# Layer two's seven products in pairs: a fourth bank, a split x-by-keys product, key sums gated on GpSimd, four kept sums moved

## The chip, the cores and the metric

One core of a Trainium2 chip runs the kernel. Its engines have queues of their own and wait for each other through semaphores: PE (TensorE; its weight loads are listed as PEld), DVE (VectorE), ACT (ScalarE), POOL (GpSimd) and SP (SyncE, which here only issues DMAs). The metric is the device time of one execution in microseconds, the median over runs. Matmul sums lie in eight PSUM banks of 128x512 float32; everything else lies in SBUF.

## What is computed

Two layers with the same weights. Each is a linear-attention block and a gated MLP with token mixing, on 2048 tokens (16 tiles of 128) of 512 features:

```python
def _A_ref(x, wqkv, wo):                       # H = 32 heads of 16
    q, k, v = ...                              # from x @ wqkv
    phi = lambda t: where(t > 0, t + 1, exp(t)) + 1e-6
    pq, pk = phi(q), phi(k)
    kv = einsum("bhsd,bhse->bhde", pk, v)
    z = einsum("bhsd->bhd", pk)
    num = einsum("bhqd,bhde->bhqe", pq, kv)
    den = einsum("bhqd,bhd->bhq", pq, z)[..., None] + 1e-6
    return (num / den) @ wo
def _B_ref(x, w_in, w_sp, b_sp, w_out):
    z = gelu(x @ w_in)
    z1, z2 = z[..., :896], layernorm(z[..., 896:])
    return (z1 * (w_sp @ z2 + b_sp)) @ w_out
x = x + _A_ref(layernorm(x), ...)
x = x + _B_ref(layernorm(x), ...)              # and both once more
```

## The kernel before

Every float32 product is done as three matmuls on high and low parts (`mm3`): high by high, high by low, low by high. A split into parts is an ACT copy that rounds (the high part, L136) and a DVE subtraction (the low part, L139). All engines follow the order in which the program is written.

The stages are, for each layer: keys, queries and the x-by-keys product (class `P1`), a transition, the rest of attention and the MLP's inputs (`P2`), and the token mixing with the output (`P4`). The change lies in layer two's `P1`, and in the loops ahead of and behind it.

**Layer two's pairs.** Tiles 0 to 9 go in five pairs (`pair`, p = 0 to 4). For a pair of tiles a and b, the product of 256 rows with the key and query weights is done by Winograd's seven products of half size, P1 to P7, each of six matmuls. Before, they use three banks: A (P1, then P2 on top), E (P7, then P4 on top) and B (an ACT copy of A, L897, then P6, P5, P3 on top). w is a copy of E taken before P4, u a copy of B taken after P6. The four quarters of keys and queries are A, X = w + B after P5 (written into bank A, L948), B after P3, and E + u (written into E, L975). From each, `pair_phi` (two ACT operations, Relu L868 and Exp L869) and `pair_out` (two DVE operations of 128x256, L879) make the key half `r` and the query half. A tile's keys are then split (`K_high` ACT L569, `K_low` DVE L574), added up on GpSimd (L578), and multiplied with the tile's x, split by `x_high` and `x_low`, in `Gmm`: twelve matmuls onto four banks G that stay through the stage. So three product banks, four G banks and one more make eight. Tiles of pair p get their `Gmm` in pair p+1. The next pair's operands are made in this pair: two stream transposes (`rows`, L448), four half-size sums (`pair_sums`), and three splits into xA (`first_part`), xB (`second_part`) and xS (`sum_part`); xD (`last_part`) is split at the pair's own start. The last of the five pairs prepares tile 10 instead, and tiles 10 to 15 follow one by one in `second`.

**Kept sums.** Token mixing's nested product N4 needs 16 sums of blocks of w_sp, made ahead of time (`Inner`), each by a DVE addition (L1694 to L1704), an ACT high part, a DVE low part and DMAs. `begin` sets how many are due, each call of `staged` moves the pipeline on by one. Eight of N4's are made in layer one's last loop (`join`, which runs once for each of 16 tiles i, at i = 3 to 6 and 12 to 15), four in pairs 1 to 4, four in layer two's mixing. The sums of N1 are made in layer two's `P2.run`, from step s = 6 on.

**Weights of P4.** In pair 0, `joint.parts(m, j, (4,))` splits the weight operand of the product P4: four ACT and four DVE operations of 128x256.

## Time and profile before

| | |
|---|---|
| median of 3 runs | 1385.57 us (1384.47 to 1385.74) |
| the profiled execution | 1386.03 us, its span 1384.0 us |
| PE busy | 1354.5 us (98%) |
| DVE busy | 1067.9 us (77%) |
| ACT busy | 658.1 us (48%) |
| POOL busy | 509.4 us (37%) |
| layer two's pairs and the hand-over to single tiles | 692.6 to 797.3 us of the span |

A row of the timeline has the start, the duration, the engine, the line, the operation, its tiles (out<-in) and shapes; in brackets stands how long the engine was idle before it and what released it. Consecutive matmuls overlap: their spacing, not their duration, is what each takes of PE. A row of the windows has a stretch and its length, then the busy time (with the number of instructions) of PE, PEld, DVE, ACT and POOL, then the granted TensorE clock, the DMA engines' busy share and GB/s.

### The profile page before, as it was taken

The numbers are of one execution on the slowest core, as the hardware profiler recorded it, in microseconds if no ns is written. First come the engines' busy times: TensorE is split into PE (matmuls) and PEld (weight loads), VectorE is DVE, ScalarE is ACT, GpSimd is POOL, SyncE is SP. The second block draws the span as 40 slices with busy tenths as digits, with TensorE's granted clock in tenths as the row PEclk, the third lists the DMA queues.
The fourth block names the chain that finished last, engine by engine and source line by source line (L and its number), as shares of the span: only waits on it lengthen the run. The fifth ranks groups of instructions, "written<-read, shape, count | busy, mean of one in ns | idle before, by whom it ended". The sixth has DMA issues, their size and how long they took to land. (4 is left out here: it accounts for less than half of the span.)

```text
span 1384.0 us, 18449 instructions
## 1 busy us (share of the span) xinstructions
PE 1354.5 (98%) x6055; PEld 1126.0 (81%) x6055; DVE 1067.9 (77%) x1670; ACT 658.1 (48%) x1066; POOL 509.4 (37%) x600
## 2 busy tenths in 40 slices
PE   9999999999999999999978899999999999999998
PEld 6888888888888888887756688888888888888887
DVE  7985887876866898978968777877777698878642
ACT  7875543345443343434456665544456534533410
POOL 3343476533483357327412224633240011312340
PEclk9999999999999999999989999999999999999999
DMA  5762479866797988869653442656567798668652
GB/s 189 230 205 88 137 258 321 294 205 207 266 333 263 311 285 283 301 257 308 223 187 101 128 147 77 217 181 226 191 204 247 232 347 312 206 197 297 230 185 88
DMA packets 181743, 310.16 MB, mean 224 GB/s; under 512 B 15696, under 2 KB 67920, under 8 KB 177552
## 3 DMA queue, kind: packets, MB, share of 16 engines
q1 hardware_dynamic: 166544, 251.45, 55.4%
q0 software_dynamic: 11504, 51.12, 10.2%
q10 hardware_dynamic: 3600, 6.42, 1.3%
q8 instruction: 47, 0.77, 0.2%
q14 instruction: 48, 0.39, 0.1%
HBM read 211.68 MB, written 97.26 MB: 223 GB/s over the span
## 5 line engine op out<-in xcount | busy, mean ns | idle before, releaser
L1973 PE MATMUL bank<-qd,pg 128*128 128x512 f32 x544 | 211.6, 389 | 0.0
L1974 PE MATMUL bank<-qd,pg 128*128 128x512 f32 x544 | 211.6, 389 | 0.0
L1975 PE MATMUL bank<-qd,pg 128*128 128x512 f32 x544 | 211.6, 389 | 0.0
L1820 DVE TENSOR_TENSOR qd<-qd,qd 128x1024 fp32r<-128x1024 f32 x104 | 140.9, 1355 | 67.8 <-ACT qd L1811 67.3
L1811 ACT ACTIVATE qd<-qd 128x1024 fp32r<-128x1024 f32 x104 | 110.1, 1058 | 129.6 <-DMA qd<-s 43.9
L136 ACT ACTIVATE pg<-pg 128x512 fp32r<-128x512 f32 (+1 forms) x146 | 88.3, 612 | 109.8 <-DVE pg L448 30.3
L380 POOL TENSOR_SCALAR rs<-mv 128x1 f32<-128x1 f32 x96 | 41.8, 436 | 258.1 <-DVE mv L375 244.2
L1995 POOL TENSOR_TENSOR bg<-bg,pg 128x512 f32<-128x512 f32 x56 | 91.2, 1641 | 109.2 <-DMA pg<-z 102.3
L139 DVE TENSOR_TENSOR pg<-pg,pg 128x512 fp32r<-128x512 f32 (+1 forms) x143 | 112.7, 789 | 20.9 <-ACT pg L136 17.9
L1974 PEld LDWEIGHTS bank<-qd,pg 128*128 128x128 f32 x544 | 102.1, 188 | 21.4
L1975 PEld LDWEIGHTS bank<-qd,pg 128*128 128x128 f32 x544 | 102.1, 188 | 21.2
L1973 PEld LDWEIGHTS bank<-qd,pg 128*128 128x128 f32 x544 | 102.1, 188 | 21.1
L152 PE MATMUL bank<-qd,pg 128*128 128x512 f32 x300 | 117.4, 391 | 0.5 <-DVE pg L139 0.5
L1563 POOL TENSOR_TENSOR pg<-pg,pg 128x512 f32<-128x512 f32 x50 | 78.3, 1567 | 104.6 <-DMA pg<-in_wsp_dram 82.1
L448 DVE STREAM_TRANSPOSE pg<-pg 128x512 f32<-128x512 f32 x79 | 86.0, 1088 | 11.3 <-DMA pg<-yt 9.5
L150 PE MATMUL bank<-bg,qd 128*128 128x448 f32 x256 | 94.0, 367 | 0.0
L151 PE MATMUL bank<-bg,qd 128*128 128x448 f32 x256 | 93.6, 366 | 0.0
L152 PE MATMUL bank<-bg,qd 128*128 128x448 f32 x256 | 93.4, 365 | 0.0
L152 PE MATMUL bank<-wo,qd 128*128 128x512 f32 x224 | 88.0, 393 | 3.2 <-DVE qd L139 3.1
L151 PE MATMUL bank<-wo,qd 128*128 128x512 f32 x224 | 87.2, 389 | 0.0
L150 PE MATMUL bank<-wo,qd 128*128 128x512 f32 x224 | 87.2, 389 | 0.0
L1904 PE MATMUL bank<-qd,pg 128*128 128x512 f32 x224 | 87.1, 389 | 0.0
(289 smaller groups left out, 3362.5 us busy)
## 6 DMA issues: line engine op xcount, KB each, us to landing
qd<-s SPq DMA_DIRECT2D x64, 512.0 KB, 4.2
qd<-n POOLq DMA_DIRECT2D x32, 1024.0 KB, 8.9
pg<-in_wsp_dram SPq DMA_DIRECT2D x96, 256.0 KB, 4.9
qd<-in_wsp_dram SPq DMA_DIRECT2D x40, 512.0 KB, 4.3
n<-pg SPq DMA_DIRECT2D x68, 256.0 KB, 4.3
pg<-z SPq DMA_DIRECT2D x56, 256.0 KB, 4.7
x<-pg SPq DMA_DIRECT2D x48, 256.0 KB, 2.9
pg<-x SPq DMA_DIRECT2D x48, 256.0 KB, 3.9
```

The costliest lines, as they stand in the source:

```text
L136: nc.scalar.activation(h, src, AF.Copy)
L139: nc.vector.tensor_sub(l, src, h.bitcast(F32))
L150: nc.tensor.matmul(out, ah, bh, start=start, stop=False)
L151: nc.tensor.matmul(out, ah, bl, start=False, stop=False)
L152: nc.tensor.matmul(out, al, bh, start=False, stop=stop)
L1811: nc.scalar.activation(wh, r, AF.Copy)
L1820: nc.vector.tensor_sub(wl, r, wh.bitcast(F32))
L1904: m(out[i], h[:, o, f], w[:, o, 0], start=first and name in ("P1", "P2", "P5"), stop=False, skip_group_check=True)
L1973: m(out, h[:, o], w[:, 0, j, :], start=start, stop=False, skip_group_check=True)
L1974: m(out, h[:, o], w[:, 1, j, :], start=False, stop=False, skip_group_check=True)
L1975: m(out, l[:, o], w[:, 0, j, :], start=False, stop=stop, skip_group_check=True)
L1995: nc.gpsimd.tensor_tensor(u, u, z1, op=OP.mult)
```

## The change

It does seven things. (1) X gets a bank of its own, so PE may write the other banks sooner; the quarter E + u goes to an SBUF tile c, and E's bank is released at once. (2) The order of the products becomes P1, P7, P2, P6, P5, P4, P3 in pairs 1 to 4 and P1, P7, P6, P2, P5, P4, P3 in pair 0: P4 stands between P5 and P3, and P3's quarter is left for the next pair. (3) `Gmm` of the tile that is finished last is cut in halves: two of its four banks between P5 and P4, the other two in the next pair between P7 and P2. (4) The key sums leave `K_low` in pairs 1 to 4; they are issued by `zsum` behind a GpSimd operation of 128x1 (`wait_for`; in pair 4 only the first of the two has one) that reads what DVE has just written, ahead of a transposition on DVE. The first transposition of a pair has the sum of tile b of the pair before, the second that of tile a. (5) The low part of a piece of the output weights goes from GpSimd (L144) to DVE. (6) P4's weight operand is split in `join` at i = 15, and tile 15's normalised rows are made and sent later in pair 0. (7) Four of N4's kept sums go from i = 3 to 6 of `join` to s = 3 to 6 of layer two's `P2.run`, and N1's start one step later there.

```diff
-        def Gmm(self, i):
+        def Gmm(self, i, cs=range(4), first=None):
...
+            if cs[-1] < 3:
+                self.xhl[i] = h, l
+                return
             pages.put(h, l, *self.pk.pop(i))
...
+        def wait_for(self, t):
+            s = small.tile([P, 1], F32, name="after")
+            nc.gpsimd.tensor_scalar(s, t if t.dtype == F32 else t.bitcast(F32), 1.0, None, op0=OP.mult)
+        def zsum(self, i):
+            r = self.r.pop(i)
+            if self.zacc is None:
+                self.zacc = r
+            else:
+                nc.gpsimd.tensor_tensor(r, self.zacc, r, op=OP.add)
+                pages.put(self.zacc, lag=POOL)
+                self.zacc = r
+        def key_low(self, i):
+            h, l = self.pk[i]
+            nc.vector.scalar_tensor_tensor(l, self.r[i], PHI_EPS, h.bitcast(F32), op0=OP.add, op1=OP.subtract)
...
             B = banks.get(PAGE)
+            if p:
+                c, r, last = self.open
+                self.pair_out(c, r, b - 2, 0)
+                self.K_high(b - 2)
             nc.scalar.activation(B, A, AF.Copy)
+            self.last_part(p)
             if p:
-                self.K_high(a - 2)
...
+                r = self.pair_phi(last)
+                self.key_low(b - 2)
+                self.x_high(b - 2)
+                self.x_low(b - 2)
...
             nc.scalar.activation(w, E, AF.Copy)
             if p:
-                self.keys(b - 2)
-            else:
-                for m in range(2):
-                    for j in range(2):
-                        self.joint.parts(m, j, (4,))
-                        self.joint.done(m, j + 2)
-            if p:
+                self.pair_out(last, r, a - 2, 1)
+                banks.put(last)
+                self.K_high(a - 2)
+                self.key_low(a - 2)
+                if p > 1:
+                    self.Gmm(a - 4, (2, 3), False)
                 self.product(A, "P2", p)
             self.product(B, "P6", p)
...
+                self.pair_out(A, r, a, 0)
+                self.Gmm(b - 2, range(4), p == 1)
+                self.x_high(a - 2)
+                self.x_low(a - 2)
+                self.wait_for(self.xhl[a - 2][1][:, 0:1])
+                self.zsum(b - 2)
...
                 self.first_part(nxt)
+                if p:
+                    self.wait_for(self.ops[nxt, "A"][1][:, 0, 0:1])
+            if p:
+                self.zsum(a - 2)
+            self.product(B, "P5", p)
+            X = banks.get(PAGE)
+            nc.vector.tensor_add(X, w, B)
+            r = self.pair_phi(X)
...
+            if p:
+                self.Gmm(a - 2, (0, 1), False)
+            lows = deque()
             if p and side:
-                side.popleft().piece(True)
+                side.popleft().piece(lows=lows)
...
+            self.product(E, "P4", p)
+            nc.vector.tensor_add(c, E, u)
+            banks.put(E)
             self.product(B, "P3", p)
-            r = self.pair_phi(B)
-            self.product(E, "P4", p)
-            self.pair_out(B, r, a, 1)
-            banks.put(B)
-            nc.vector.tensor_add(E, E, u)
-            self.open = E, b
+            self.open = c, self.pair_phi(c), B
+            for l, src, h, t in lows:
+                low(l, src, h)
+                pages.put(t)
+            own.staged(False)
...
-                elif s == 5:
-                    own.begin(2)
-                elif 6 <= s:
-                    own.staged()
+                else:
+                    if s == 2:
+                        inner["N4"].begin(1, 1)
+                    elif 2 < s < 10:
+                        inner["N4"].staged(s < 7)
+                    if s == 6:
+                        own.begin(2)
+                    elif s > 6:
+                        own.staged()
...
-            if i == 2:
-                inner["N4"].begin(2, 1)
-            elif 2 < i < 10 or i > 11:
-                inner["N4"].staged(i < 7 or i > 11)
+            if i == 11:
+                inner["N4"].begin(1, 1)
+            elif i > 11:
+                inner["N4"].staged()
+            if i == 15:
+                for m in range(2):
+                    for j in range(2):
+                        w.parts(m, j, (4,))
+                        w.done(m, j + 2)
```

Three places of the engines' orders follow. ACT at the start of pair 0, before (L897 is the copy of A to B, bg and qd of 128x256 are P4's weight parts, w and u the copies of E and B):

```order
L136 ACTIVATE pg_730_7025<-pg_719_6890 128x512
L897 ACTIVATE bank_182_7047<-bank_180_7033 128x512
L394 ACTIVATE pg_733_7049<-pg_720_6892,nb,rs 128x4x4x32
L136 ACTIVATE pg_734_7051<-pg_710_6782 128x256
L136 ACTIVATE qd_159_7028<-pg_728_6983 128x512
L915 ACTIVATE w_7060<-bank_181_7040 128x512
L136 ACTIVATE qd_160_7062<-pg_665_6275 128x256
L136 ACTIVATE qd_160_7062<-pg_679_6395 128x256
L136 ACTIVATE qd_160_7062<-pg_666_6277 128x4x2x32
L136 ACTIVATE qd_160_7062<-pg_680_6397 128x4x2x32
L931 ACTIVATE u_7077<-bank_182_7047 128x512
L868 ACTIVATE pg_735_7085<-bank_180_7033 128x512
```

and now (L922 is the copy of A to B, L930 writes w, L951 u, L871 is the Relu):

```order
L136 ACTIVATE pg_720_6991<-pg_709_6856 128x512
L136 ACTIVATE qd_159_6994<-pg_665_6275 128x256
L136 ACTIVATE qd_159_6994<-pg_677_6391 128x256
L136 ACTIVATE qd_159_6994<-pg_666_6277 128x4x2x32
L136 ACTIVATE qd_159_6994<-pg_678_6393 128x4x2x32
L922 ACTIVATE bank_182_7022<-bank_180_7008 128x512
L136 ACTIVATE pg_723_7024<-pg_698_6744 128x256
L930 ACTIVATE w_7027<-bank_181_7015 128x512
L951 ACTIVATE u_7035<-bank_182_7022 128x512
L871 ACTIVATE pg_724_7043<-bank_180_7008 128x512
```

The four parts of P4's weights moved from between w and u to ahead of the copy of A; tile 15's normalisation (L394) and a kept sum's high part (qd of 128x512) left this place. ACT at the start of pair 2, before (bank_185 and bank_192 are B of pairs 1 and 2):

```order
L868 ACTIVATE pg_774_7308<-bank_185_7176 128x512
L869 ACTIVATE pg_774_7308<-pg_774_7308 128x512
L897 ACTIVATE bank_192_7340<-bank_190_7326 128x512
L569 ACTIVATE pg_778_7342<-pg_760_7220 128x512
L136 ACTIVATE pg_780_7345<-pg_763_7244 128x256
```

and now (c is E + u of pair 1, bank_186 its B):

```order
L871 ACTIVATE pg_763_7280<-c_7272 128x512
L872 ACTIVATE pg_763_7280<-pg_763_7280 128x512
L569 ACTIVATE pg_768_7309<-pg_759_7251 128x512
L922 ACTIVATE bank_194_7306<-bank_192_7292 128x512
L136 ACTIVATE pg_770_7313<-pg_753_7211 128x256
L871 ACTIVATE pg_771_7316<-bank_186_7142 128x512
L872 ACTIVATE pg_771_7316<-pg_771_7316 128x512
```

The Relu and Exp of the old B moved behind the copy, those of c ahead of it, and the key's high part (L569) now stands ahead of the copy. GpSimd from pair 1 on, before (L144 is the weights' low part):

```order
L578 TENSOR_TENSOR pg_743_7122<-pg_736_7088,pg_743_7122 128x512
L144 TENSOR_TENSOR bg_14_7281<-pg_748_7156,bg_13_7280 128x512
L578 TENSOR_TENSOR pg_760_7220<-pg_743_7122,pg_760_7220 128x512
L578 TENSOR_TENSOR pg_769_7286<-pg_760_7220,pg_769_7286 128x512
L144 TENSOR_TENSOR bg_14_7281<-pg_775_7320,bg_13_7280 128x512
```

and now:

```order
L892 TENSOR_SCALAR after<-pg_752_7206 128x1
L892 TENSOR_SCALAR after<-pg_754_7215 128x1
L899 TENSOR_TENSOR pg_725_7046<-pg_733_7086,pg_725_7046 128x512
L892 TENSOR_SCALAR after<-pg_779_7372 128x1
L899 TENSOR_TENSOR pg_759_7251<-pg_725_7046,pg_759_7251 128x512
```

The weights' low parts are gone from it, and each key sum has an operation of one column ahead of it.

72 lines of the change are left out of this document (28 added, 44 removed).

## The prediction

> **What bounds the kernel now.** I read the page's totals first, then PE's waits, then busy time by stage. The number of matmuls does not change, so the time moves only by what PE idles and by the clock it gets.
>
> ```profile
> PE   1354.5 (98%) x6055; PEld 1126.0 (81%) x6055; DVE 1067.9 (77%) x1670; ACT 658.1 (48%) x1066; POOL 509.4 (37%) x600
> ...
> PE bank L802 <- DVE bank L948: 9.4, 4, 6.7
> PE bank L152 <- DVE pg L139: 5.3, 5, 1.5
> ...
> PE bank L802 <- ACT u L931: 2.2, 1, 2.2
> ```
>
> Some 29.5 us of 1384.0 are not PE's. The waits (us in total, times, longest) name the place: L802 is a matmul of the seven products, L948 the addition that makes X, L931 the copy u of pair 0, L152 (here) the third matmul of a `Gmm` or of a tile's keys. The windows give it by stage; the rows are layer one's last loop, pairs 0, 1, 2 and 3, pair 4 with the hand-over, the rest, and steps 3 to 5 of layer two's `P2`.
>
> ```profile
> 634.00:692.60 58.60, 55.41 (x237) 43.61 (x236) 53.56 (x93) 27.07 (x42) 30.53 (x39) 1.00 0.76 252
> 692.60:714.40 21.80, 12.93 (x44) 9.59 (x43) 14.14 (x28) 12.17 (x22) 1.90 (x4) 0.70 0.78 263
> 714.40:731.10 16.70, 15.79 (x67) 12.51 (x66) 11.82 (x22) 10.18 (x20) 2.30 (x2) 0.98 0.29 97
> 731.10:749.50 18.40, 15.92 (x68) 12.17 (x67) 15.82 (x27) 11.29 (x22) 3.91 (x4) 1.00 0.32 101
> 749.50:767.90 18.40, 15.84 (x67) 12.14 (x66) 15.76 (x27) 11.19 (x22) 3.79 (x4) 1.00 0.33 101
> 767.90:797.30 29.40, 24.95 (x104) 18.76 (x103) 23.12 (x37) 18.44 (x35) 6.80 (x6) 1.00 0.41 124
> 797.30:1384.00 586.70, 582.41 (x2637) 489.64 (x2635) 433.70 (x703) 256.02 (x413) 155.05 (x190) 1.00 0.63 211
> 863.50:887.00 23.50, 23.50 (x115) 20.48 (x114) 21.32 (x41) 12.41 (x21) 15.97 (x21) 1.00 0.66 207
> ```
>
> PE idles 3.2 us in the loop, 8.9 in pair 0 (at a clock of 0.70), then 0.9, 2.5, 2.6 and 4.5: 22.6 us. In pairs 2 and 3 neither PE nor DVE (15.8 of 18.4 us) is full: their length is set by a chain that goes to and fro between DVE and ACT, each in the program's order. So I lay that chain out anew, with durations from rows.
>
> **Layer one's loop: four kept sums leave.**
>
> ```profile
> 634.46 0.68 DVE L1694 TENSOR_TENSOR pg<-pg,pg 128x512 f32<-128x512 f32 x1
> ```
>
> Each sum takes an addition like this one and a low part of the same size, from a stretch where DVE is busy 53.6 of 58.6 us: 8 x 0.60 (their spacing, below) = 4.8 us of work leave, against 3.2 us of idle PE. ACT highs and DMAs leave too. Four later sums stay, and P4's weight parts come in at the loop's end, so I leave 0.4 us of waits: **-2.8 us**, bounds 0 and -3.2.
>
> **Pair 0.**
>
> ```profile
> 692.61 0.39 PE L802 MATMUL bank<-qd,xA 128*128 128x512 f32 x1
> ...
> 694.18 0.58 ACT L897 ACTIVATE bank<-bank 128x512 f32<-128x512 f32 x1
> ...
> 698.54 1.32 ACT L136 ACTIVATE qd<-pg 128x256 fp32r<-128x256 f32 x4
> ...
> 700.85 1.28 ACT L869 ACT_TABLE_LOAD   x1
> ...
> 702.81 0.42 DVE L879 SCALAR_TENSOR_TENSOR pg<-bank,pg 128x256 f32<-128x256 f32 x1 [2.40 <-ACT pg L869]
> ...
> 703.48 1.07 DVE L448 STREAM_TRANSPOSE pg<-pg 128x512 f32<-128x512 f32 x1
> ...
> 708.36 0.69 DVE L948 TENSOR_TENSOR bank<-w,bank 128x512 f32<-128x512 f32 x1
> ```
>
> On before's clock: P4's four weight highs now run 694.2 to 695.5 ahead of the copy, which ends at 696.1 (before 694.8). P7 ends at 695.3, so P6 waits 0.7 us. P6 (six matmuls at 0.23) ends at 697.6, u comes right behind it, P2 runs on without a wait to 698.9, then Relu (0.6), the table load (1.28) and Exp (0.63): `pair_out` starts at 701.6, 1.2 us earlier. From there to X it was 5.55 us. The second transposition, two half-size sums and a kept sum's low part now stand behind X, and 3.05 us are left: two halves (0.68), a transposition with its high part (1.76) and a low part (0.60). X starts at 704.6 instead of 708.36. PE has P4 in hand until 701.6 and then waits 3.8 us instead of 6.7; the 2.2 us at u go. The clock will probably fall again, but PE has time to spare there.
>
> From X on, DVE does what it put off (transposition 1.11, four half sums 1.6, kept low 0.6, two halves 0.7, xB and xS lows 1.2, another kept low 0.6, c 0.7), and ACT Relu and Exp of c (1.3): pair 1's `pair_out` of c starts at 713.0.
>
> **A steady pair.** Spacings come from these rows: 0.60 for a DVE operation of 128x512, 0.52 and 0.30 for ACT of 128x512 and 128x256, 0.62 from Relu to Exp, 0.03 from ACT's end to DVE's start.
>
> ```profile
> 734.40 0.62 ACT L569 ACTIVATE pg<-pg 128x512 fp32r<-128x512 f32 x1
> 734.92 0.41 ACT L136 ACTIVATE pg<-pg 128x256 fp32r<-128x256 f32 x1
> 735.22 0.59 ACT L868 ACTIVATE pg<-bank 128x512 f32<-128x512 f32 x1
> 735.84 0.64 ACT L869 ACTIVATE pg<-pg 128x512 f32<-128x512 f32 x1
> ...
> 735.36 0.43 DVE L139 TENSOR_TENSOR pg<-pg,pg 128x256 fp32r<-128x256 f32 x1 [0.94 <-ACT pg L136]
> ...
> 743.36 0.69 DVE L139 TENSOR_TENSOR pg<-pg,xA 128x512 fp32r<-128x512 f32 x1 [0.70 <-ACT xA L136]
> ...
> 727.51 0.69 DVE L948 TENSOR_TENSOR bank<-w,bank 128x512 f32<-128x512 f32 x1
> ...
> 745.88 0.69 DVE L948 TENSOR_TENSOR bank<-w,bank 128x512 f32<-128x512 f32 x1
> 746.48 0.42 DVE L842 TENSOR_TENSOR pg<-pg,pg 128x256 f32<-128x256 f32 x1
> ...
> 764.31 0.69 DVE L948 TENSOR_TENSOR bank<-w,bank 128x512 f32<-128x512 f32 x1
> ```
>
> X to X took 18.37 and 18.43 us. DVE also loses time to GpSimd:
>
> ```profile
> 730.09 1.29 POOL L144 TENSOR_TENSOR bg<-pg,bg 128x512 fp32r<-128x512 f32 x1 [7.40 <-ACT bg L136]
> ...
> 730.57 1.37 DVE L139 TENSOR_TENSOR pg<-pg,xB 128x512 fp32r<-128x512 f32 x1 [0.29 <-ACT xB L136]
> ...
> 737.21 1.28 POOL L578 TENSOR_TENSOR pg<-pg,pg 128x512 f32<-128x512 f32 x1 [5.82 <-ACT pg L136]
> ...
> 737.57 1.47 DVE L139 TENSOR_TENSOR pg<-pg,pg 128x512 fp32r<-128x512 f32 x1
> ...
> 95.19 1.10 DVE L448 STREAM_TRANSPOSE pg<-pg 128x512 f32<-128x512 f32 x1
> ...
> 95.36 1.29 POOL L578 TENSOR_TENSOR pg<-pg,pg 128x512 f32<-128x512 f32 x1 [1.76 <-DVE pg L574]
> ```
>
> A subtraction of two SBUF tiles that meets a GpSimd sum ends 0.55 us after that sum: 1.37 to 1.47 us instead of 0.69. A transposition beside one takes its usual 1.1 (layer one). Key sums beside transpositions thus save 2 x 0.75 us of DVE in a pair; the weights' low part on DVE costs 0.60, about the stall that it caused.
>
> Now the chain, t = 0 at `pair_out` of c. DVE's work: eight halves of `pair_out` 2.7, xD's low 0.34, ten operations on keys, x, next operands, weights and kept sum 6.0, X and c 1.2, two transpositions 2.2, four half sums 1.6: 14.1 us. Its idle time, where ACT's order makes it wait: xD's low part stands behind the key's high part (0.47), the copy of A (0.99) and xD's high part (to 1.90), idle 1.25; `x_low` of b-2 behind Relu, Exp and a high part, idle 0.73; the key's low part of a-2, 0.44; `pair_out` of A (Exp ends 6.45), 0.57; `x_low` of a-2, 0.31; xA's low part, 0.70 as in the row; c's Exp, 0.22. That is 4.2 us: **18.3 us a pair**, X at 10.5. What GpSimd no longer takes from DVE comes back as waits for ACT, since K, copy, Relu and Exp now stand ahead of nearly every DVE operation in the pair's first half. PE needs 66 x 0.227 = 15.0 us and idles 3.3: at P7's third matmul for xB's low part (1.4), and at P2 for the copy of A (1.9), although half a `Gmm` lies ahead of it.
>
> So X of pair 1 comes at 713.0 + 10.5 = 723.5 instead of 727.51, **-4.0 us**; pairs 2 and 3 give **-0.2**.
>
> `wait_for` is not in the trace; the nearest is
>
> ```profile
> 692.64 0.27 POOL L384 TENSOR_SCALAR nb<-mv,rs 128x1 f32<-128x1 f32 x1
> ```
>
> 0.3 to 0.5 us while DVE transposes. Then the first sum runs 8.7 to 10.0 and the second 11.1 to 12.4 in t, and each only brushes the operation behind its transposition (xA's low at 9.9, the half sums at 12.2). Bounds: 0, and 1.3 us for `wait_for`, as long as a sum, with a full collision each.
>
> **Pair 4 and the hand-over.**
>
> ```profile
> 797.29 0.39 PE L150 MATMUL bank<-qd,z_h 128*128 128x512 f32 x1
> ```
>
> This starts tile 11's keys; from it on PE hardly stops. X of pair 3 to here was 33.0 us. Laid out: X of pair 4 at 9.2 (no xA), c at 12.5, lows to 14.3, `pair_out` of c 14.5, tile 9's key low 16.2 (behind both Relu-Exp pairs), its x low 17.5, the transposition 18.7, tile 8's x low 21.1 to 21.7; its `Gmm` ends at 24.0. From X of pair 3 that is 18.3 - 10.5 + 24.0 = 31.8: **-1.2**.
>
> **Layer two's `P2`.** Four kept sums come in, 4 x 1.2 = 4.8 us of DVE in steps 3 to 7, where it idles 2.2 us in 23.5.
>
> ```profile
> 876.99 0.69 DVE L1200 TENSOR_TENSOR pg<-pg,bank 128x512 f32<-128x512 f32 x1 [1.09 <-PE bank L152]
> ```
>
> DVE waits for PE there, not PE for DVE, and its low parts are for the next step's matmuls. N1's first addition leaves step 6. I take 0; the bound is what doesn't fit, +2.6.
>
> **The sum.** -2.8 - 4.0 - 0.2 - 1.2 = -8.2; 0.4 us back for a clock that may still be low when pair 1's P2 comes: -7.8. The profiled execution took 1386.03 (span 1384.0 and 2.0 around it), which gives 1378.2; it stands 0.46 above the median, so 1377.8 beside 1385.57. I say **1378.0**, own range 1374.5 to 1381.5, chance 0.55.
>
> **Rivals.**
>
> *GpSimd's sums still collide* (0.15). If `wait_for` takes a microsecond, both sums hit subtractions again: 0.78 x 2 x 3.5 pairs = +5.5, 1383.5. For: GpSimd's one-column operations vary. Against: they run beside an operation that left GpSimd alone in layer one.
>
> *`P2` pays for the four sums* (0.10): +2.6, 1380.6. For: DVE is 91% busy there. Against: PE never waits in it.
>
> *The waits for ACT are shorter than I laid out* (0.08). If half of the 4.2 us goes in four pairs, -8: 1370. PE's own 15.0 us is the floor.
>
> *Slower: the clock falls in every pair* (0.12). The matmuls behind the gap at u:
>
> ```profile
> 701.80 0.63 PE L804 MATMUL bank<-bg,pg 128*128 128x512 f32 x1
> ```
>
> Its successors were 0.43 us apart, not 0.23, until 715, some 14 of them. The gap ahead was only 2.2 us, and each new pair has gaps of 1.4 and 1.9. Two falls in a pair cost 2 x 14 x 0.2 = 5.6 us, of which PE has 1.9 to spare before X (P5 ends at 8.6, X starts at 10.5): +3.7 x 4 pairs, 1393. It decides from 2 us a pair on. Against: the gaps of 0.9 to 1.5 us in pairs 1 to 4 left the clock at 1.00. The Trainium skill (TensorE: Matmul & The Clock Gate, Part 1: The HAM clock gate) has the array fall to half clock after an idle window of about 3.4 us; by that no pair but 0 loses it. This trace shows a fall after 2.2 us of idleness, so the rule is no safeguard here.
>
> **How the numbers follow.** A run can tell about 0.2% (2.8 us) from no change: faster is below 1382.8, slower above 1388.3. Faster gets nearly all of the forecast, of `P2` and of shorter waits, and a quarter of the collisions: 0.75. Same is most of the collisions, 0.12; slower the clock, 0.13. For 8 in 10 the range goes from 1372 (shorter waits in part) to 1385.5 (collisions).
>
> **What would show it.** Right: L152's wait for qd gone in the loop; X of pair 0 about 3.8 us earlier relative to the pair's first matmul, one PE gap of about 4 us; X to X of 18 to 18.6; PE waiting at P2 for ACT's copy and at P7 for a low part; transpositions of 1.1 beside sums, no L139 at 1.4. Wrong: X to X under 17 or over 19.5, PE clock below 1.00 in pairs 2 to 4, or idle PE after 797.

## The result, and the profile after

The changed kernel takes 1376.7 us (median; 1375.74 to 1379.56) beside 1385.02 for the kernel before: a ratio of 0.9943, 95% interval 0.9926 to 0.996. The profiled executions read 1375.74 (span 1374.0) and 1386.03 (1384.0). Of the 10.0 us between these spans, 0.7 had come about in code that is the same in both; the medians are 8.3 apart.

The page's totals and the list of PE's waits (us in total, times, longest):

```profile
PE 1351.4 (98%) x6055; PEld 1127.4 (82%) x6055; DVE 1062.0 (77%) x1674; ACT 659.2 (48%) x1066; POOL 506.5 (37%) x603
```

```profile
PE bank L805 <- ACT bank L922: 8.4, 5, 3.4
PE bank L805 <- DVE bank L967: 3.7, 1, 3.7
PE bank L805 <- ACT pg L136: 2.1, 2, 1.1
...
PE bank L152 <- DVE pg L139: 1.5, 1, 1.5
```

Two lines of the same list in before, beside those that the prediction shows:

```profile
PE bank L152 <- DVE qd L139: 3.1, 4, 1.5
...
PE bank L802 <- ACT bank L897: 1.7, 3, 0.6
```

L967 is X, L922 the copy of A. X made PE wait four times for 9.4 us, and now once for 3.7; L152's waits fell from 5.3 and 3.1 to 1.5; u is gone from the list. In their place stand the copy of A, 8.4 us in five pairs where it was 1.7 in three, and P7 of pairs 3 and 4 (2.1). The rows for pair 3's P7:

```profile
740.33 0.41 DVE L882 SCALAR_TENSOR_TENSOR z_q<-bank,pg 128x256 f32<-128x256 f32 x1
...
740.89 0.47 PE L805 MATMUL bank<-bg,xB 128*128 128x512 f32 x1 [1.08 <-ACT pg L136]
```

The row names a high part of a kept sum (L136), which P7 does not read. By the order in which the program hands out banks, P7 writes into the bank that held X of the pair before, and `pair_out` of X (L882) ends 0.15 us before P7 starts, here, in pair 4 and in both pairs of the run a_ungated; the operation that the row names ends 0.01 to 0.10 us before it. So it is most likely X's bank that P7 waits for.

By the busy column PE idles 22.6 us of the span, where it idled 29.5.

The windows: layer one's last loop up to pair 0, pairs 0 to 3 (each up to the next pair's `pair_out` of c), pair 4 with the hand-over, and all that follows.

```profile
628.00:686.60 58.60, 58.60 (x260) 48.54 (x259) 52.50 (x92) 27.81 (x42) 34.49 (x44) 1.00 0.71 228
686.60:707.10 20.50, 14.68 (x56) 10.99 (x54) 13.75 (x27) 12.31 (x22) 2.16 (x4) 0.92 0.55 172
707.10:725.50 18.40, 16.69 (x66) 13.45 (x66) 14.47 (x27) 11.81 (x22) 1.72 (x3) 0.91 0.60 209
725.50:743.90 18.40, 15.88 (x67) 12.07 (x66) 14.48 (x27) 11.76 (x21) 2.95 (x4) 1.00 0.30 90
743.90:762.30 18.40, 15.78 (x67) 12.08 (x66) 14.47 (x27) 11.76 (x21) 2.93 (x4) 1.00 0.37 110
762.30:787.40 25.10, 21.64 (x91) 16.75 (x91) 19.15 (x34) 17.40 (x32) 5.75 (x5) 1.00 0.52 148
787.40:1374.00 586.60, 582.34 (x2637) 489.64 (x2635) 435.47 (x711) 257.56 (x417) 156.82 (x190) 1.00 0.64 216
```

The loop's 58.6 us hold 260 matmuls, where 237 stood before: no idle PE is left. Pairs 2 and 3 take 18.4 us as before, with DVE down from 15.8 to 14.5 us of work: it waits 1.3 us longer in each, as was laid out. What follows the hand-over holds 4.3 us of idle PE, as before.

The timeline: the pair's first matmul, the additions that make X (pairs 0 to 3), a key sum beside a transposition, and tile 11's first matmul.

```profile
686.70 0.39 PE L805 MATMUL bank<-qd,xA 128*128 128x512 f32 x1
...
698.74 0.69 DVE L967 TENSOR_TENSOR bank<-w,bank 128x512 f32<-128x512 f32 x1
717.65 0.69 DVE L967 TENSOR_TENSOR bank<-w,bank 128x512 f32<-128x512 f32 x1
736.05 0.69 DVE L967 TENSOR_TENSOR bank<-w,bank 128x512 f32<-128x512 f32 x1
...
736.39 1.30 POOL L899 TENSOR_TENSOR pg<-pg,pg 128x512 f32<-128x512 f32 x1
736.65 1.11 DVE L448 STREAM_TRANSPOSE pg<-pg 128x512 f32<-128x512 f32 x1
...
754.47 0.69 DVE L967 TENSOR_TENSOR bank<-w,bank 128x512 f32<-128x512 f32 x1
...
787.40 0.39 PE L150 MATMUL bank<-qd,z_h 128*128 128x512 f32 x1
```

All kernels of this study by such rows (us; "first" is pair 0's first matmul; X1-X0 and so on are distances of the rows of X, "hand-over" goes from X of pair 4 to tile 11's first matmul). A median stands beside that of the kernel before in the same session.

| kernel | median / before | first | X0 - first | X1-X0 | X2-X1 | X3-X2 | X4-X3 | hand-over |
|---|---|---|---|---|---|---|---|---|
| before | 1385.02 | 692.61 | 15.75 | 19.15 | 18.37 | 18.43 | 15.66 | 17.32 |
| changed | 1376.7 / 1385.02 | 686.70 | 12.04 | 18.91 | 18.40 | 18.42 | 16.99 | 15.94 |
| b_sums | 1379.26 / 1385.51 | 686.51 | 15.76 | 19.07 | 18.46 | 18.41 | 15.61 | 17.31 |
| b_p4w | 1384.08 / 1385.51 | 691.90 | 14.80 | 17.94 | 18.41 | 18.42 | 15.66 | 18.03 |
| a_ungated | 1379.05 / 1385.51 | 687.14 | 12.04 | 18.93 | 19.14 | 19.10 | 17.69 | 15.86 |
| a_copy_first | 1375.05 / 1385.51 | 689.56 | 12.02 | 18.37 | 17.82 | 17.82 | 16.39 | 15.94 |
| a_tail | 1375.9 / 1384.9 | 687.33 | 12.03 | 18.90 | 18.43 | 18.40 | 16.99 | 15.13 |
| a_table | 1376.37 / 1384.9 | 687.93 | 11.36 | 19.93 | 18.41 | 18.42 | 17.00 | 15.93 |
| b_xfirst | 1381.31 / 1384.9 | 691.49 | 12.28 | 19.22 | 18.41 | 18.36 | 15.62 | 17.32 |
| a_chain | 1368.51 / 1384.9 | 687.16 | 12.05 | 16.82 | 16.17 | 16.17 | 15.54 | 15.87 |
| a_sums_back | 1382.07 / 1385.15 | 692.80 | 12.11 | 18.94 | 18.42 | 18.42 | 17.00 | 15.94 |
| best1 | 1367.27 / 1385.15 | 688.08 | 12.03 | 17.09 | 16.19 | 16.16 | 15.55 | 14.23 |
| best2 | 1366.67 / 1385.15 | 687.08 | 10.77 | 17.67 | 16.19 | 16.18 | 15.54 | 14.24 |
| b_min | 1377.28 / 1384.94 | 688.30 | 12.29 | 18.36 | 18.50 | 18.38 | 15.63 | 17.31 |

"First" also carries what the code ahead happened to take: a_copy_first, whose code up to there is that of the changed kernel, comes 2.9 us later, 1.8 of it before 600 us and 1.0 at two matmuls between 601 and 606 us that waited for a DMA. The distances do not have this, and the readings below use them or a lead measured on both sides of a stage.

### The profile page after: what moved, and what is told of

Same layout as the page of the kernel before. It is cut to its first block, busy times and chain, and to the rows that moved or that the text cites. A ratio compares the mean times of both kernels' runs of the same rounds, so it can differ in the third digit from the quotient of the medians.

```text
span 1374.0 us, 18443 instructions
## 1 busy us (share of the span) xinstructions
PE 1351.4 (98%) x6055; PEld 1127.4 (82%) x6055; DVE 1062.0 (77%) x1674; ACT 659.2 (48%) x1066; POOL 506.5 (37%) x603
## 4 chain that ended last, share of the span: by engine, by line
PE 91%; DVE 4%; ACT 3%; issue 1%; DMA 1%; SPq 0%; POOL 0%; DVEq 0%; ACTq 0%; POOLq 0%
PE bank L152 16%; PE bank L151 16%; PE bank L150 16%; PE bank L2010 9%; PE bank L2011 9%; PE bank L2009 9%; PE bank L1942 4%; PE bank L1940 4%; PE bank L1943 4%; PE bank L1380 1%; PE bank L1379 1%; PE bank L1378 1%; DVE pg L139 1%; DVE pg L448 1%; PE bank L404 1%
## 5 line engine op out<-in xcount | busy, mean ns | idle before, releaser
L2009 PE MATMUL bank<-qd,pg 128*128 128x512 f32 x544 | 211.6, 389 | 0.0
L2010 PE MATMUL bank<-qd,pg 128*128 128x512 f32 x544 | 211.6, 389 | 0.0
L2011 PE MATMUL bank<-qd,pg 128*128 128x512 f32 x544 | 211.6, 389 | 0.0
L1856 DVE TENSOR_TENSOR qd<-qd,qd 128x1024 fp32r<-128x1024 f32 x104 | 144.3, 1388 | 61.1 <-ACT qd L1847 60.4
L136 ACT ACTIVATE pg<-pg 128x512 fp32r<-128x512 f32 (+1 forms) x146 | 88.5, 613 | 118.7 <-DVE pg L448 37.2
L139 DVE TENSOR_TENSOR pg<-pg,pg 128x512 fp32r<-128x512 f32 (+1 forms) x143 | 105.3, 737 | 20.2 <-ACT pg L136 16.4
L152 PE MATMUL bank<-qd,pg 128*128 128x512 f32 x300 | 117.4, 391 | 0.0
L152 PE MATMUL bank<-bg,qd 128*128 128x448 f32 x256 | 93.4, 365 | 0.0
L1940 PE MATMUL bank<-qd,pg 128*128 128x512 f32 x224 | 87.1, 389 | 0.0
L1942 PE MATMUL bank<-qd,pg 128*128 128x512 f32 x224 | 87.1, 389 | 0.0
L1943 PE MATMUL bank<-qd,pg 128*128 128x512 f32 x224 | 87.1, 389 | 0.0
L150 PE MATMUL bank<-wo,qd 128*128 128x512 f32 x224 | 87.1, 389 | 0.0
```

Source lines behind the costliest of these rows:

```text
L139: nc.vector.tensor_sub(l, src, h.bitcast(F32))
L150: nc.tensor.matmul(out, ah, bh, start=start, stop=False)
L152: nc.tensor.matmul(out, al, bh, start=False, stop=stop)
L1856: nc.vector.tensor_sub(wl, r, wh.bitcast(F32))
L1940: m(out[i], h[:, o, f], w[:, o, 0], start=first and name in ("P1", "P2", "P5"), stop=False, skip_group_check=True)
L1942: m(out[i], h[:, o, f], w[:, o, 1], start=False, stop=False, skip_group_check=True)
```

## The experiments

### The loop: kept sums moved alone, and moved back

b_sums is the kernel before with part 7 alone; a_sums_back is the changed kernel with part 7 undone.

```diff
 # P2.run, layer two
-                elif s == 5:
-                    own.begin(2)
-                elif 6 <= s:
-                    own.staged()
+                else:
+                    if s == 2:
+                        inner["N4"].begin(1, 1)
+                    elif 2 < s < 10:
+                        inner["N4"].staged(s < 7)
+                    if s == 6:
+                        own.begin(2)
+                    elif s > 6:
+                        own.staged()
 # join
-            if i == 2:
-                inner["N4"].begin(2, 1)
-            elif 2 < i < 10 or i > 11:
-                inner["N4"].staged(i < 7 or i > 11)
+            if i == 11:
+                inner["N4"].begin(1, 1)
+            elif i > 11:
+                inner["N4"].staged()
```

> The kernel before with part 7 alone: four of N4's kept sums go from layer one's last loop to layer two's P2. Theory A (PE's real idle time is read from the number of its matmuls: 237 x 0.227 = 53.8 of 58.6 us, so 4.8 idle, which the sums cause): pair 0's first matmul comes 4.8 to 5.3 us earlier than in the kernel before, the total falls by about 5, to 1380. Theory B (idle time as the busy column gives it, 3.2, as I predicted): 2.8 earlier, 1382.2. Theory C (part 7 only pushes the work into layer two's P2): the lead of 5 shrinks by 1 to 3 us between steps 3 and 7 of P2, 1381 to 1383.

> The changed kernel with part 7 undone: the four kept sums are made again in layer one's last loop. Theory A (the loop's gain is the sums' alone and stands beside the rest of the change): pair 0's first matmul comes 5 to 6 us later than in the changed kernel, and the time is 5 to 6 us longer, 1382. Theory B (pair 0 hides part of it, or the loop's gain came from what else left it): 2.8 longer, 1379.5. What layer two's P2 does without the four sums is seen in the lead between 850 and 950 us: Theory A has no dip there.

Measured: -6.25 us for the sums alone, +5.4 for their return (1376.7 to 1382.07). The windows of the same ten microseconds of the loop, in before and in b_sums:

```profile
645.00:655.00 10.00, 8.46 (x36) 6.54 (x36) 9.72 (x18) 4.14 (x6) 4.89 (x7) 1.00 0.62 197
```

```profile
645.00:655.00 10.00, 10.00 (x45) 8.26 (x44) 9.13 (x19) 4.71 (x8) 4.72 (x7) 1.00 0.59 186
```

36 matmuls against 45. The busy column shows 1.5 us of idleness in the first row; 36 x 0.227 = 8.2 us of matmuls leave 1.8. Over the whole loop the lead of b_sums over before (between equal DVE rows of the two) goes from 0.9 at 600 us to 6.2 at 680, which is 5.3, and a_sums_back loses the same 5.3 against the changed kernel (0.9 behind at 620, 6.2 at 680). The 0.9 comes from ahead of the loop. That is theory A in both: the sums alone, by the number of matmuls.

What P2 pays is seen in three equal DVE rows, ahead of the moved sums, among them and behind them, in the changed kernel and then in a_sums_back:

```profile
836.83 0.35 DVE L1190 RECIPROCAL den<-den 128x32 f32<-128x32 f32 x1
...
896.16 0.69 DVE L139 TENSOR_TENSOR qd<-pg,qd 128x512 fp32r<-128x512 f32 x1 [1.50 <-ACT qd L136]
...
938.69 0.68 DVE L1231 TENSOR_TENSOR pg<-pg,bank 128x512 f32<-128x512 f32 x1
```

```profile
843.07 0.35 DVE L1190 RECIPROCAL den<-den 128x32 f32<-128x32 f32 x1
...
899.53 0.69 DVE L139 TENSOR_TENSOR qd<-pg,qd 128x512 fp32r<-128x512 f32 x1 [1.50 <-ACT qd L136]
...
944.74 0.68 DVE L1231 TENSOR_TENSOR pg<-pg,bank 128x512 f32<-128x512 f32 x1
```

The distance is 6.24 us, then 3.37, then 6.05: with four more sums DVE falls 2.9 us behind and catches up to 0.2, and from 1000 us on the distance is 6.2 again. Moving the sums cost P2 nothing that stayed.

### Pair 0: the weights alone, and X ahead of the second transposition

b_p4w moves the weight split alone; b_xfirst adds to it, in pair 0, P5 and X ahead of the second transposition.

```diff
 # pair
             if p:
                 self.keys(b - 2)
-            else:
-                for m in range(2):
-                    for j in range(2):
-                        self.joint.parts(m, j, (4,))
-                        self.joint.done(m, j + 2)
 ...
                 self.first_part(nxt)
+                if p == 0:                          # b_xfirst only
+                    self.product(B, "P5", p)
+                    nc.vector.tensor_add(A, w, B)
+                    r = self.pair_phi(A)
                 self.rows(b + 2)
 # join
+            if i == 15:
+                for m in range(2):
+                    for j in range(2):
+                        w.parts(m, j, (4,))
+                        w.done(m, j + 2)
```

> The kernel before with one piece of part 6 alone: P4's weight operand is split in layer one's last loop at i = 15 instead of between w and u of pair 0. Theory A: u is no longer late, PE's wait for u (2.2) goes and X of pair 0 comes 1.2 us earlier after the pair's first matmul (14.5 instead of 15.75); the other 2.5 us that pair 0 won come from what now stands behind X. The loop, still full, pays up to 1 us for the eight operations: total -0.3 to -1.2, 1384 to 1384.7. Theory B: u was the whole of it: X after 12 us, total -3.7, 1381.3. Theory C: the loop pays as much as pair 0 wins: no change, X at 14.5 but the first matmul 1 us later.

> The kernel with P4's weight split alone (b_p4w), and in pair 0 P5 and X ahead of the second transposition. Theory A (the rest of pair 0's gain is that DVE makes X before the second transposition, two half sums and a kept sum's low part, 2.5 us): X of pair 0 at 12.3 us after the pair's first matmul instead of 14.8, but pair 1's gain is smaller by what DVE then does later; total 1381.5 to 1382.5. Theory B (it needs X's own bank or the order P5, P4, P3): X at 14.8, total 1384.

Measured: -1.4 us (ratio 0.999, interval 0.9981 to 1.0, at the edge of no change) and -3.6. X of pair 0 comes 0.95 us sooner with the weights moved (14.80 after the first matmul instead of 15.75), and 2.52 sooner again with X ahead of the transposition (12.28): together 3.47 of the 3.71 that the whole change won there. The loop paid nothing for the eight operations (lead 0.6 at 600 us and 0.7 at 680). Theory A held in both, with 0.95 us for the weights where it said 1.2.

b_p4w also gained 1.2 us between X of pair 0 and of pair 1, which no theory had. The timeline's row of its copy of A in pair 1, and that of before:

```profile
713.44 0.58 ACT L897 ACTIVATE bank<-bank 128x512 f32<-128x512 f32 x1 [1.77 <-PE bank L804]
```

```profile
716.31 0.58 ACT L897 ACTIVATE bank<-bank 128x512 f32<-128x512 f32 x1 [2.98 <-PE bank L804]
```

In before the copy waits 2.98 us for PE and comes 7.95 us after X (716.31 - 708.36); in b_p4w 6.74. PE's matmuls ahead of it ran at half clock, in before for much longer; the last section has the rows. At the hand-over b_p4w lost 0.7, with the clock at half there.

### The gates on the key sums

```diff
 # pair, p >= 1
                 self.x_low(a - 2)
-                self.wait_for(self.xhl[a - 2][1][:, 0:1])
                 self.zsum(b - 2)
 ...
                 self.first_part(nxt)
-                if p:
-                    self.wait_for(self.ops[nxt, "A"][1][:, 0, 0:1])
```

> The changed kernel without its two GpSimd operations of one column, so that the key sums start as soon as GpSimd is free and the keys are there. Theory A (the gates are what keeps the sums beside transpositions): the sum of tile b starts beside an x_low or another subtraction and that takes 1.4 instead of 0.69, 0.6 us a pair on the chain; X to X about 19.0 instead of 18.4, total +2 to +2.5, 1379. Theory B (both sums collide and everything collided is on the chain): +1.5 a pair, +5 in all, 1382. Theory C (the chain waits for ACT there anyway): X to X 18.4, no change, 1376.7.

Measured: 1379.05 us in place of 1376.7; X to X 19.1 in place of 18.4, from pair 2 on, and 2.1 us over all distances of the table. The timeline of pair 2 in a_ungated:

```profile
729.22 1.30 POOL L899 TENSOR_TENSOR pg<-pg,pg 128x512 f32<-128x512 f32 x1 [14.12 <-PE bank L807]
...
729.54 1.52 DVE L139 TENSOR_TENSOR pg<-pg,pg 128x512 fp32r<-128x512 f32 x1 [0.64 <-ACT pg L136]
```

The first sum starts under x's low part, which takes 1.52 us instead of 0.69: 0.7 us a pair, once in each pair from the second on. The other sum, from 732.94 to 734.23, ended just ahead of the next subtraction (734.26, 0.69 us). Theory A, one collision a pair; the operation of one column that avoids it takes 0.21 us of GpSimd in the changed kernel.

### What bounds a steady pair

a_copy_first puts the copy of A and xD's high part ahead, and leaves DVE's order as it is. a_chain changes the order of ACT further, and puts two DVE operations of tile a elsewhere, the key's low part and x's low part (`x_low` now ahead of `pair_out` of A); neither adds nor removes work.

```diff
 # a_copy_first
             B = banks.get(PAGE)
+            nc.scalar.activation(B, A, AF.Copy)
+            self.last_high(p)
             if p:
                 c, r, last = self.open
                 self.pair_out(c, r, b - 2, 0)
                 self.K_high(b - 2)
-            nc.scalar.activation(B, A, AF.Copy)
-            self.last_part(p)
+            self.last_low(p)
 # a_chain, on top of it
             if p:
+                self.x_high(b - 2)
                 r = self.pair_phi(last)
                 self.key_low(b - 2)
-                self.x_high(b - 2)
                 self.x_low(b - 2)
+                self.x_high(a - 2)
+                self.pair_out(last, r, a - 2, 1)
+                banks.put(last)
             w = ...
-            nc.scalar.activation(w, E, AF.Copy)
+            if p == 0:
+                nc.scalar.activation(w, E, AF.Copy)
             if p:
-                self.pair_out(last, r, a - 2, 1)
-                banks.put(last)
-                self.K_high(a - 2)
-                self.key_low(a - 2)
 ...
                 r = self.pair_phi(A)
+                self.K_high(a - 2)
                 nc.scalar.activation(u, B, AF.Copy)
+                nc.scalar.activation(w, E, AF.Copy)
+                self.x_low(a - 2)
                 self.pair_out(A, r, a, 0)
                 self.Gmm(b - 2, range(4), p == 1)
-                self.x_high(a - 2)
-                self.x_low(a - 2)
-                self.wait_for(self.xhl[a - 2][1][:, 0:1])
+                self.wait_for(self.r[a][:, 0:1])
                 self.zsum(b - 2)
 ...
                 self.turn.row(a + 2)
+                self.key_low(a - 2)
             else:
                 self.rows(a + 2)
-                self.first_part(nxt)
+                self.part_high(nxt, "A", self.y[2 * nxt], self.tags(nxt)[0])
+                if p:
+                    self.key_low(a - 2)
+                self.part_low(nxt, "A", self.y[2 * nxt])
```

> The changed kernel with ACT's copy of A and xD's high part ahead of pair_out of c and the key's high part. It tells what bounds a steady pair of the changed kernel. Theory A (the chain between DVE and ACT, in program order, as laid out: DVE's idle time of 1.2 us at xD's low part shrinks to 0.6): X to X 17.8 instead of 18.4, PE's wait at P2 for the copy about 0.5 instead of 1.5, total -2 to -2.4, 1374.5. Theory B (PE's waits at P2 and P7 bound the pair, 1.5 of them at P2): X to X about 17.0, total -5, 1372. Theory C (the time lost only moves: the delayed key's high part makes key_low and x_low later): X to X 18.4, no change, 1376.7.

> The kernel with the copy of A first (a_copy_first), and in pairs 1 to 4 ACT's order changed again: x's high part of tile b ahead of the old B's Relu and Exp; x's high part of tile a, then Relu and Exp of A, then tile a's key high part, u and w; on DVE tile a's key low part goes between the transposition and xA's low part. DVE has the same work; only what it waits for changes. Theory A (the pair is a chain between DVE and ACT in program order, laid out with rows): x low of b waits no more (0.6 less), pair_out of A comes 1.4 earlier, key low fills the wait for xA's high part; X to X about 15.8 instead of 17.8, total -8 to -10 against the changed kernel, 1367 to 1369. Theory B (PE's own 15.0 us and its waits at P7 and P2 bind first): X to X 16.5 to 17.2, 1370 to 1372. Theory C (DVE is what is full, and the waits only move): X to X 17.8, 1375.

Measured: X to X 17.82 with the copy first (2.3 us over four distances; 1375.05), and 16.17 with the whole order (8.1 over all distances; 1368.51, a ratio to before of 0.9883, interval 0.9868 to 0.9898). The windows of pair 3 from X to X, in the changed kernel and in a_chain:

```profile
736.05:754.47 18.42, 15.79 (x68) 12.09 (x67) 14.48 (x28) 11.77 (x21) 2.93 (x4) 1.00 0.39 115
```

```profile
732.20:748.37 16.17, 15.71 (x67) 11.98 (x67) 14.57 (x29) 11.66 (x21) 2.99 (x4) 1.00 0.40 130
```

DVE has 14.5 us of work in both, ACT 11.7; what went are DVE's waits for ACT. In a_chain PE's 67 matmuls, 15.2 us at 0.227, leave it 1.0 us of 16.2. Theory A in both, a little short in the second: 16.17 for 15.8 (theory B began at 16.5). The rest is a wait that the layout did not have: the Relu of A waits 0.38 us for `pair_out` of the old B, most likely for the page that this frees.

```profile
743.92 0.60 ACT L875 ACTIVATE pg<-bank 128x512 f32<-128x512 f32 x1 [0.38 <-DVE z_q L886]
...
745.22 0.42 DVE L886 SCALAR_TENSOR_TENSOR pg<-bank,pg 128x256 f32<-128x256 f32 x1 [0.81 <-ACT pg L876]
```

It is half of the 0.81 us for which DVE then waits at `pair_out` of A.

### The hand-over

a_tail gives the hand-over's two key sums gates as well:

```diff
 # second, first
-                    self.keys(s - 2)
+                    self.K_high(s - 2)
+                    self.key_low(s - 2)
                     self.pair_out(last, r, s - 3, 1)
                     banks.put(last)
                     self.xsplit(s - 2)
-                    self.keys(s - 3)
+                    self.K_high(s - 3)
+                    self.key_low(s - 3)
+                    self.wait_for(self.pk[s - 3][1][:, 0:1])
+                    self.zsum(s - 2)
 ...
                     self.xsplit(s - 1)
+                    self.wait_for(self.xhl[s - 1][1][:, 0:1])
+                    self.zsum(s - 3)
```

> The changed kernel with the two key sums of the hand-over (tiles 9 and 8) also behind a GpSimd operation of one column: the first waits for tile 8's key low part and so runs beside the transposition, the second waits for tile 10's x low part. Theory A (my hand-over term failed because the sum that has no gate meets tile 9's x low part, 1.46 us instead of 0.69): that low part takes 0.7, tile 11's keys start 0.7 to 0.8 us earlier after the pairs' last X, total -0.7, 1376.0. Theory B (the wait for the key's high part and the transposition bound it, the collision is beside the path): no change, 1376.7, with the idle time moved in front of the transposition's high part.

The place in the changed kernel (GpSimd's sum, tile 9's x low part, the transposition), and then in a_tail:

```profile
779.45 1.27 POOL L578 TENSOR_TENSOR pg<-pg,pg 128x512 f32<-128x512 f32 x1 [5.49 <-PE bank L152]
...
779.81 1.46 DVE L139 TENSOR_TENSOR pg<-pg,pg 128x512 fp32r<-128x512 f32 x1
781.79 1.08 DVE L448 STREAM_TRANSPOSE pg<-pg 128x512 f32<-128x512 f32 x1
```

```profile
780.42 0.68 DVE L139 TENSOR_TENSOR pg<-pg,pg 128x512 fp32r<-128x512 f32 x1
781.62 1.08 DVE L448 STREAM_TRANSPOSE pg<-pg 128x512 f32<-128x512 f32 x1
...
782.03 1.29 POOL L899 TENSOR_TENSOR pg<-pg,pg 128x512 f32<-128x512 f32 x1
```

The low part takes 0.68 instead of 1.46, the sum runs beside the transposition, and tile 11's keys come 15.13 us after the last X instead of 15.94: 0.8, theory A. The time, 1375.9 beside 1376.7, agrees with it, though a difference of that size is within what the medians scatter.

best1 joins this to a_chain, with tile 8's low part ahead of the transposed tile's:

```diff
+                    self.x_high(s - 3)
                     self.T_high(s)
+                    self.x_low(s - 3)
                     self.T_low(s)
                     self.Gmm(s - 2)
-                    self.xsplit(s - 3)
                     self.xsplit(s - 1)
```

> The kernel with the changed order of ACT (a_chain), the two gates of the hand-over (a_tail), and tile 8's x high part ahead of, its low part right behind, the transposition there. Theory A (the gains are separate: 0.75 for the gate, 0.6 for the low part that no longer stands behind the transposition's): tile 11's keys come 14.5 us after the last X instead of 15.9, total -1.3 against a_chain, 1367.2. Theory B (PE's Gmm of tile 9, then of tile 8, bind the hand-over): -0.5, 1368.

The hand-over takes 14.23 us and the kernel 1367.27 (ratio 0.9867, interval 0.9852 to 0.9882): theory A.

### The table load

```diff
 # join, a_table
+            if i == 14:
+                e = small.tile([P, 1], F32, name="exp")
+                nc.scalar.activation(e, nxt.ms[i][2], AF.Exp)
 # join, best2, on top of best1
+            if i == 13:
+                e = small.tile([P, 1], F32, name="exp")
+                nc.scalar.activation(e, mhalf[:, 0:1], AF.Exp)
```

> The changed kernel with one small Exp (one column, result unused) on ACT in layer one's last loop, at i = 14, so that the table load of 1.28 us leaves pair 0's chain from Relu to Exp. Theory A (pair 0 is set by the chain P2, Relu, table, Exp, pair_out, transposition, X): X of pair 0 comes 10.75 us after the pair's first matmul instead of 12.04, PE's gap there is 2.4 instead of 3.7, total -1.3, 1375.4; if the gap is then too short for the clock to fall, up to 0.5 more. Theory B (X of pair 0 is set by PE's P5): X at 12.0, no change. Theory C (what pair 0 gains is lost to the chain of pair 1): X to X of pair 1 grows from 18.9 to about 20, no change in the total.

> best1 with a small Exp on a constant column in layer one's last loop at i = 13, where it waits for nothing, so that the table load leaves pair 0. Theory A: X of pair 0 comes 10.75 us after the pair's first matmul instead of 12.05, total -1.3 against best1, 1366. Theory B (as in a_table: the gap moves, the clock is low during pair 1's P1 and P7 and the copy behind them comes late): X of pair 0 earlier by 1.3, X to X of pair 1 longer by 1, total -0.3.

a_table: 1376.37, no change. X of pair 0 came only 0.7 sooner, since the small Exp waited 1.31 us for GpSimd's statistics and everything behind it on ACT was later; and pair 1 took 1.0 us longer, theory C. Its u had to wait for PE, as the timeline of a_table shows, and behind that row stands the window of its low clock:

```profile
714.87 0.60 ACT L943 ACTIVATE u<-bank 128x512 f32<-128x512 f32 x1 [0.70 <-PE bank L807]
```

```profile
708.30:715.20 6.90, 5.85 (x14) 4.60 (x15) 4.01 (x9) 5.52 (x11) 0.00 (x0) 0.51 0.79 287
```

The clock was at half for these 6.9 us, in which pair 1's P2 and P6 fall; in the changed kernel a spell of 3.4 us lies there. best2, whose Exp waits for nothing, has X of pair 0 at 10.77, 1.26 sooner than best1, and loses 0.6 of it in pair 1 (17.67 for 17.09). Its median, 1366.67, is 0.6 below best1's, between its theories A and B, but its runs (1365.94 to 1368.75) hold best1's (1367.0 to 1367.56): whether it is faster stays open.

### What the reordered pairs bring

b_min has the edits of b_xfirst and of b_sums together, as they stand above: no fourth bank, no split `Gmm`, no gates, and no new order in pairs 1 to 4.

> The kernel before with part 7, P4's weight split in layer one's last loop, and in pair 0 alone P5 and X ahead of the second transposition; pairs 1 to 4 keep their order, their three banks and their ungated key sums. Theory A (the reordered pairs 1 to 4 of the change give nothing on balance, as X to X of 18.4 in both says): 5.3 from the loop and 3.5 from pair 0 and the start of pair 1, less what the hand-over pays: total -8 to -9.5 against the kernel before, 1376 to 1377, as the changed kernel. Theory B (the changed pairs bring some of the gain): 1378 to 1380.

Measured: 1377.28 us beside 1384.94 (ratio 0.9948, interval 0.9934 to 0.9961), against 0.9943 for the whole change. X to X is 18.4 to 18.5 as in both. Theory A: pairs 1 to 4 as the change writes them gave nothing on balance, to within about a microsecond. For pair 1 takes 18.36 us here and 19.22 in b_xfirst, with the same code: there its copy of A waited 2.62 us for PE, here 1.77, and the spell of half clock lay 1.9 us later after the pair's first matmul than here.

## Why the prediction was right

1378.0 was forecast and 1376.7 measured. Term by term, with the distances of the table:

- **The loop: -2.8 forecast (bounds 0 and -3.2), -5.3 measured.** One of two terms that were mis-sized by more than a little, and the measured value lies outside its bounds. The mechanism was right: L152's wait for qd is gone, and the sums alone do it. The size came from the busy column: 58.60 - 55.41 = 3.2 us of idle PE. But the records of consecutive matmuls overlap, 0.39 us long at a spacing of 0.227, so each gap looks 0.16 us shorter than it is. By count, 237 x 0.227 = 53.8, the idle time is 4.8; against the 260 matmuls of the changed kernel's full loop 23 are missing, 5.2 us. The 0.4 us of waits that I left for what stays were not there either.
- **Pair 0: X 3.8 us earlier forecast, 3.71 measured**, 0.95 of it the weights' (1.2 forecast) and 2.5 the order on DVE (2.5 forecast). One gap of 3.7 us stands in PE's waits (3.8 forecast), and P6 waits for the copy.
- **X of pair 1: -4.0 forecast, -3.95 measured** (34.90 after the first matmul before, 30.95 now). The 0.4 us that I gave back for a low clock was not paid in the changed kernel: the clock fell twice, but the chain, not PE, set X of pair 1. That it can be paid, a_table shows.
- **Steady pairs: 18.3 forecast, 18.40 and 18.42 measured** (18.37 and 18.43 before). The reason was that DVE's work falls by 1.3 us and its waits for ACT grow by as much. In pair 2 of the changed kernel the seven waits that I had laid out took 1.18, 0.64, 0.37, 0.46, 0.25, 0.77 and 0.17 us, 3.8 where I had 4.2. a_copy_first and a_chain settle it: the same work takes 17.8 with ACT's order alone changed, and 16.2 with ACT's changed further and two DVE operations moved. a_ungated shows what the gates saved, 0.7 a pair, and that without them the new order takes 19.1, 0.7 more than before; b_min, that the two together brought nothing. One reading was wrong beside this: I had PE wait at P7's third matmul for xB's low part, and it waited at the first, most likely for X's bank.
- **The hand-over: -1.2 forecast, -0.05 measured** (32.98 to 32.93 from X of pair 3 to tile 11's keys). X of pair 4 came 17.0 after that of pair 3, as laid out; the error lies behind it, 15.9 us where I had 14.8. I had counted the pairs' key sums as gated and overlooked that `second` issues its own without a gate, and the first of these met an x low part as in the kernel before (tile 9's took 1.46 us; before, tile 8's took 1.41). a_tail gets back 0.8 of the 1.15; the other 0.35 has no single place.
- **`P2`: 0 forecast, 0 measured.** DVE fell 2.9 us behind, and PE did not wait.

The sum that was measured in these places is -5.3 - 3.95 - 0.05, and nothing for the steady pairs: -9.3, where I had -7.8. The loop's 2.5 more, the hand-over's 1.15 less, the 0.2 that the steady pairs did not give and the 0.4 that the clock did not take make up the difference. The profiled executions' further 0.7 comes from ahead of the loop. The medians show 8.3, 1.0 less than these places, from kernels whose runs spread over 1.3 us (before) and 3.8 us (changed). That the forecast came so close is partly luck: its two mis-sized terms had opposite signs.

Of the rivals, GpSimd's collisions did not come in the pairs, because the operation of one column took 0.21 us; where no gate stood, at the hand-over, they did. `P2` did not pay. The clock did fall, but in pairs 0 and 1 alone; pairs 2 to 4, with waits of PE of 1.1 and some 1.5 us in them, kept 1.00; the last section has what decides. That ACT's waits could be made shorter was true, but by another order, which the change does not have.

## What to carry to other kernels

Read PE's idle time from the number of matmuls times their spacing, not from the busy column, where overlapping records hide a part of every gap. Where two engines hand work to and fro in program order, lay out both queues with durations from rows: taking work from the busier one gains nothing while the other's order sets the waits, and reordering, with no work removed, was worth 8 us on top of a change whose own new order had brought nothing in the same pairs: 2.3 from the other engine's order alone, the rest from more of it with two operations of the busier one moved. When a fix is put into one place, look for the same instruction in the code that follows it: the sum at the hand-over kept the collision that the pairs had lost.

## What the runs showed of the hardware

The low clock comes in spells of one length or its multiples. The windows below, of before, of the changed kernel and of b_p4w, are stretches with the clock at half (the third number from the end of a row); just outside them it reads 1.00.

```profile
701.50:715.10 13.60, 6.92 (x17) 4.95 (x16) 9.41 (x18) 5.39 (x9) 0.00 (x0) 0.50 0.70 238
```

```profile
699.80:703.20 3.40, 3.40 (x9) 2.63 (x8) 3.30 (x8) 3.15 (x6) 0.00 (x0) 0.50 0.09 25
710.00:713.40 3.40, 3.40 (x9) 2.66 (x9) 2.20 (x5) 2.76 (x6) 0.00 (x0) 0.51 0.92 333
```

```profile
704.10:710.90 6.80, 3.46 (x8) 2.79 (x9) 5.93 (x12) 2.76 (x5) 0.00 (x0) 0.50 0.62 187
789.40:792.80 3.40, 3.40 (x10) 2.62 (x9) 2.52 (x4) 2.71 (x6) 1.12 (x1) 0.50 0.00 0
```

They last 3.4, 6.8 and 13.6 us, one, two and four times 3.4. The Trainium skill (TensorE: Matmul & The Clock Gate, Part 1: The HAM clock gate) tells of a free-running activity window of about 3.4 us; these lengths agree with it. Its condition for a fall, one idle window of 3.4 us, does not hold here: in before the clock fell at 701.5, when PE had stood still for some 2.4 us of the 3.4 ahead of it (between its matmuls at 697.82 and 700.40). And in b_p4w it fell behind two short gaps at the hand-over; in before the same two gaps left it at 1.00. The rows are b_p4w's, then before's:

```profile
786.26 0.50 PE L150 MATMUL bank<-pg,pg 128*128 128x512 f32 x1 [1.00 <-ACT pg L136]
...
788.45 0.50 PE L152 MATMUL bank<-pg,pg 128*128 128x512 f32 x1 [1.47 <-DVE pg L139]
```

```profile
789.09 0.50 PE L150 MATMUL bank<-pg,pg 128*128 128x512 f32 x1 [1.00 <-ACT pg L136]
...
791.29 0.50 PE L152 MATMUL bank<-pg,pg 128*128 128x512 f32 x1 [1.47 <-DVE pg L139]
```

The spells of one trace lie on one grid: the two of the changed kernel start 10.2 us apart, three times 3.41, and the two of b_p4w 85.3, twenty-five times. Divide a trace into the windows of that grid, and count as idle what the distance of two matmuls exceeds 0.227 us by. Then b_p4w's two gaps lie in one window (786.00 to 789.41, 2.1 us idle), and before's are shared out over two (1.85 and 1.2 us). In the fourteen traces, from 20 to 1340 us, each of the twenty windows at full clock with 2.0 us or more of idle PE (the least is 2.00, in a_tail) was followed by the half clock, and none with less was (the most is 1.96, in b_xfirst). So how a gap lies to the window decides, which a small shift of the code ahead can change: 0.7 us lost at b_p4w's hand-over, 1.2 us won in its pair 1, 1.0 us lost in a_table's. Differences of about a microsecond between such kernels have to be looked up in the clock before they are put down to an edit.
